# K and V blocks in two transfers of 32 KB runs on two queues, and b1 in one transfer

## The chip, the cores and the metric

The kernel runs on one core of one Trainium2 chip. The metric is device time in microseconds for one execution; the kernel before was timed three times, with a median of 723.58 us (723.52 to 723.64). A profile of one more execution stands beside these times. In it, PE is TensorE's matmul side and PEld its weight loads, DVE is VectorE, ACT ScalarE, POOL GpSimd and SP SyncE; SPq and ACTq are the sequencers of SyncE and ScalarE, which issue transfers. A core has 16 DMA engines, which all transfers share.

## The reference

One decode step, for two sequences (B = 2), of an attention block and an MLP, mixed by a gate. Everything is float32.

```python
def reference(A_x, A_k_cache, A_v_cache, A_wq, A_wo, B_x, B_w1, B_b1, B_w2, B_b2, gate_w):
    x = A_x                                        # (2, 1, 576)
    g = _sigmoid((x * gate_w).sum(-1, keepdims=True))
    a = _A_ref(x, A_k_cache, A_v_cache, A_wq, A_wo)
    b = _B_ref(x, B_w1, B_b1, B_w2, B_b2)
    return g * a + (1 - g) * b

# _A_ref: 32 heads of 128, 4096 cached positions
q = (x @ wq).reshape(B, Sq, H, Dh)                 # then transposed to heads first
scores = einsum("bhqd,bhkd->bhqk", q, k_cache) * (Dh ** -0.5)
o = einsum("bhqk,bhkd->bhqd", softmax(scores), v_cache)
return o.reshape(B, Sq, H * Dh) @ wo

# _B_ref: 576 -> 4608 -> 576
return gelu_tanh(x @ w1 + b1) @ w2 + b2
```

The K cache and the V cache are 134 MB each; the weights are 9.4 MB for wq and for wo, 10.6 MB for w1 and for w2.

## The kernel before

**The blocks.** The 64 pairs of sequence and head are worked off in 16 blocks of four heads of one sequence (NQ = 16, HQ = 4). A block of K or V is 8.39 MB: 128 partitions with 65,536 contiguous bytes each, 32 partitions to a head, 128 positions to a partition. SBUF holds three buffers of that size: slots 0 and 1 take the K blocks in turn, slot 2 takes every V block. At the start and the end the same slots hold the weights.

**What each engine does for a block i.** VectorE multiplies K by the query row in place (L357), sums over the head size (L359, both of some 17 us) and finds the largest score (L360 to L362); this is `qk(i)`. ScalarE takes the exponentials into `pt` (L369, `soft(i)`). TensorE multiplies them by V in 32 steps (L388, in a loop over the blocks). ScalarE copies the sums out of PSUM (L377, into `avs`), TensorE combines them (L393, L395), and ScalarE copies the result into `oS` (L381); these two copies are `gather(i)`.

**Who orders the work.** The order is written out by hand. The class `Order` keeps counting semaphores for each engine and puts waits ahead of an operation (L66, L78); transfers that go through its method `dma` have the line L84. A few semaphores are handled directly: `exps` (exponentials ready), `vin` (V landed), `avd` (V's products done), `avc` and `cmb` (for the two copies), `ksem` (K landed).

**The order of the transfers.** Before the blocks, SyncE issues wq, the rest of wq, and w1 in three pieces. Then comes `k_load(0)`, which loads the first K as two transfers of half a row each, 32,768 bytes to a partition, so that VectorE can begin on the first half; each half has its own semaphore. `k_load(1)` follows when w1 in slot 1 has been used, and the first V when the MLP's activation no longer needs slot 2. In the loop of the blocks SyncE issues K of block i + 2 when `qk(i)` has finished with its slot, and V of block i + 1 when `avd` says that block i is done with slot 2. All of these are single transfers of whole rows on SyncE's queue. The weights w2 and wo follow in the same queue: most of w2 goes into slot 0 ahead of the last V, most of wo and the rest of w2 into slot 1 after the last K has been used, and the last rows of wo into slot 2 after the last V.

**ScalarE's queue** carries only small inputs: x, the gate's weights, b1 and b2 at the start, and half of the output at the end. b1 (4608 numbers, 36 to each of 128 partitions, in `b1T`) comes as 16 transfers of 15, 14, ... 1 and 8 partitions (L142 to L146), which share one semaphore. b2 comes last of these; TensorE needs it to begin the accumulation of the output (L271), ahead of the MLP's first product (L286, L295). The MLP's activation ends with a tanh on ScalarE (L315) and three steps on VectorE, and VectorE then starts on the first K.

Of the kernel before, what the change touches and what calls it, by code (L numbers as in the profile page):

```python
# [9 lines left out]
P = 128  # L10


class Order:
# [50 lines left out]
    def op(self, e, f, r=(), w=(), extra=(), sig=None):  # L64

        self.wait(e, self.deps(r, w) + list(extra))  # L66
        ins = f(self.eng[e])
        if sig is not None:
            ins.then_inc(sig, 1)
            return None  # L70
        self.count[e] += 1
        ins.then_inc(self.sem[e], 1)
        t = self.token(e, self.sem[e], self.count[e])
        self.note(t, r, w)
        return t

    def dma(self, e, out, in_, r=(), w=(), extra=(), sem=None, val=16):
        self.wait(e, self.deps(r, w) + list(extra))  # L78
        if sem is None and self.spare:
            sem, val = self.spare.pop(0)  # L80
        elif sem is None:
            sem = self.tc.alloc_semaphore(f"d{self.nd}")
            self.nd += 1
        self.eng[e].dma_start(out, in_).then_inc(sem, 16)  # L84
        t = (None, sem, val, dict(self.seen[e]))
        self.note(t, r, w)
        return t


def kernel(tc, *args):  # L90
    with tc.tile_critical():
        stored = body(tc, *args)

    with tc.tile_critical():
        for own, sem, val, had in stored:
            tc.nc.sync.wait_ge(sem, val)


def body(tc, x, k_cache, v_cache, wq, wo, w1, b1, w2, b2, gate_w, out):
    nc = tc.nc  # L100
    B, H, SK, DH = k_cache.shape
# [12 lines left out]
    FR = F // P  # L114
# [8 lines left out]
    def sb(name, *shape):  # L123
        return nc.alloc_sbuf_tensor(name, list(shape), F32).ap()

    slots = [sb(f"slot{i}", P, SLOT) for i in range(3)]
# [4 lines left out]
    o = Order(tc)  # L131
    op, dma = o.op, o.dma
    S2 = ["s2a", "s2h", "s2r", "s2t", "xg", "b2r", "xe", "g1z"]


    b1T = sb("b1T", P, FR)
    spare = slots[2][:, 2 * F + 2 * FJ:]
    xg, spare = spare[:B + 1, :D], spare[:, D:]
    b2r, spare = spare[:1, :D], spare[:, D:]
    dma("ACT", xg[:B], x.rearrange("b s d -> (b s) d"), w=["xg"])  # L140
    dma("ACT", xg[B:B + 1], gate_w[None, :], w=["gt_in"])
    b1v, b1sem, at = b1.rearrange("(p r) -> p r", r=FR), tc.alloc_semaphore("b1"), 0  # L142
    b1runs = list(range(15, 0, -1)) + [8]
    for i, n in enumerate(b1runs):
        dma("ACT", b1T[at:at + n], b1v[at:at + n], w=[f"b1T{i}"], sem=b1sem, val=16 * len(b1runs))
        at += n  # L146
    dma("ACT", b2r, b2[None, :], w=["b2r"])


# [6 lines left out]
    dma("SP", slots[2][:, :F], hrow1[:, FA * F:], w=["s2a"])  # L156
    w1h = slots[2][:, F:F + F // 2]
    dma("SP", w1h, w1[XR:].rearrange("q (e n) -> (q e) n", e=2), w=["s2h"])
    early = [o.wrote[k][0][1] for k in ("xg", "gt_in", "b2r", "s0", "s1q", "s1a", "s2a", "s2h")]
    hr = slots[2][:, 2 * F:2 * F + FJ]  # L160
    ht = slots[2][:, 2 * F + FJ:2 * F + 2 * FJ]

    def quad(src, i):
        g, b = divmod(i, B)
        return src[b, g * HQ:(g + 1) * HQ].rearrange("h (p r) d -> (h p) (r d)", p=HP)
# [58 lines left out]
    V = "DVE"  # L224
# [78 lines left out]
    for m, k in enumerate(("avp", "cps", "fin")):  # L303
        op("ACT", lambda e, m=m: e.copy(hr[:, m * FC:(m + 1) * FC], hps[m][:, :FC]), r=[k], w=[f"s2r{m}"])  # L304
    hb = sb("hb", P, FR, B)
# [2 lines left out]
    op(V, lambda e: e.transpose(ht.rearrange("p (r i) -> p r i", i=32), hr.rearrange("p (i r) -> p r i", r=FR)),  # L308
       r=["s2r0", "s2r1", "s2r2"], w=["s2t"])
    htv = ht.rearrange("p (r i) -> p r i", i=32)[:, :, :B]  # L310
    op(V, lambda e: e.tensor_add(hb, htv, b1T.unsqueeze(2).to_broadcast([P, FR, B])), r=["s2t"] + [f"b1T{i}" for i in range(len(b1runs))], w=["hb"])
    op(V, lambda e: e.tensor_mul(gt, hb, hb), r=["hb"], w=["gt"])
    op(V, lambda e: e.tensor_scalar(gt, gt, 0.044715, 1.0, op0=ALU.mult, op1=ALU.add), r=["gt"], w=["gt"])
    op(V, lambda e: e.tensor_mul(gt, gt, hb), r=["gt", "hb"], w=["gt"])
# [14 lines left out]
    vin = tc.alloc_semaphore("vin")  # L329
    avc = tc.alloc_semaphore("avc")  # L330
    avd = tc.alloc_semaphore("avd")
    cmb = tc.alloc_semaphore("cmb")
    ksem = [tc.alloc_semaphore(f"k{j}") for j in range(2)]
    done = lambda sem, val: ("PE", sem, val, {})

    RH = R // 2
    k0b = tc.alloc_semaphore("k0b")

    def k_load(i):
        s = i % 2  # L340
        if i == 0:
            free = o.deps([], ["s0"])
            for a, sem in ((0, ksem[0]), (1, k0b)):
                c = slice(a * RH * DH, (a + 1) * RH * DH)
                dma("SP", slots[0][:, c], quad(k_cache, 0)[:, c], w=[f"s0{a}"], extra=free, sem=sem)
            return
        w = ["s0"] if s == 0 else ["s1a", "s1q", "s1"]
        dma("SP", slots[s], quad(k_cache, i), w=w, sem=ksem[s], val=16 * (i // 2 + 1))

    def qk(i):  # L350
        g, b = divmod(i, B)
        s, j = ("s0", 0) if i % 2 == 0 else ("s1", 1)
        k = slots[i % 2].rearrange("p (r d) -> p r d", d=DH)
        q = qps[b][g // 4][:, (g % 4) * DH:(g % 4 + 1) * DH]
        parts = [(0, R, s)] if i else [(0, RH, "s00"), (RH, R, "s01")]
        for lo, hi, key in parts:
            op(V, lambda e, lo=lo, hi=hi: e.tensor_mul(  # L357
                k[:, lo:hi], k[:, lo:hi], q.unsqueeze(1).to_broadcast([P, hi - lo, DH])), r=["q", key], w=[key])
        op(V, lambda e: e.tensor_reduce(stt[j], k, AX.X, ALU.add), r=[s] + [p[2] for p in parts], w=[f"st{j}"])  # L359
        op(V, lambda e: e.tensor_reduce(mxt, stt[j], AX.X, ALU.max), r=[f"st{j}"], w=["mx"])  # L360
        op(V, lambda e: e.transpose(mtt, mxt.to_broadcast([P, 32])), r=["mx"], w=["mt"])
        op(V, lambda e: e.tensor_reduce(nmt[j], mtt, AX.X, ALU.max, negate=True), r=["mt"], w=[f"nm{j}"])  # L362

    def soft(i):
        j = i % 2
        o.wait("ACT", o.deps([f"nm{j}", f"st{j}"], ["pt", "rs"]))
        for h in range(HQ):
            a = slice(HP * h, HP * (h + 1))
            ins = nc.scalar.activation(pt[a, h:R * HQ:HQ], stt[j][a], AF.Exp, bias=nmt[j][a], accum_out=rs[a])  # L369
        ins.then_inc(exps, 1)  # L370

    def gather(i):

        g, b = divmod(i, B)
        j = i % 2
        nc.scalar.wait_ge(avd, i + 1)
        nc.scalar.copy(avs, avp).then_inc(avc, 1)  # L377
        a = slice(32 * (g // 2), 32 * (g // 2) + 32)
        nc.scalar.wait_ge(cmb, i + 1)

        op("ACT", lambda e: e.copy(oS[a, b, g % 2], cps[a, :DH + 1]), r=[f"st{j}", f"nm{j}"], w=[f"oS{i}"])  # L381

    def quad_products(e, v, vin):
        e.wait_ge(exps, 1).then_inc(exps, -1)
        e.wait_ge(vin, 16).then_inc(vin, -16)  # L385
        for t in range(NT):
            j = t % 4
            ins = e.matmul(avp[32 * j:32 * j + 32], pt[:, 16 * t:16 * t + 32], v[:, 512 * t:512 * (t + 1)],  # L388
                           start=(t < 4), stop=(t >= NT - 4))
        ins.then_inc(avd, 1)  # L390
        e.wait_ge(avc, 1).then_inc(avc, -1)  # L391
        for rr in range(4):
            e.matmul(cps[:, :DH], sel[:, rr], avs[:, rr * DH:(rr + 1) * DH],  # L393
                     start=(rr == 0), stop=(rr == 3), skip_group_check=True)
        e.matmul(cps[:, DH:DH + 1], hsel, rs, start=False, stop=True, skip_group_check=True).then_inc(cmb, 1)  # L395
# [6 lines left out]
    def load_rows(name, lo, hi, s, at, **kw):  # L402
        t = slots[s][:, at * D:(at + hi - lo) * D]
        dma("SP", t, views[name][:, lo * D:hi * D], w=[(name, lo)], **kw)
        for r in range(lo, hi):
            wrow[name, r] = t[:, (r - lo) * D:(r - lo + 1) * D], (name, lo)


    k_load(0)
    k_load(1)  # L410
    o.wait("SP", o.deps([], S2 + ["gt_in", "s2r0", "s2r1", "s2r2"]))
    nc.sync.dma_start(slots[2], quad(v_cache, 0)).then_inc(vin, 16)
    for i in range(NQ):
        qk(i)
        if i < NQ - 2:
            k_load(i + 2)
        elif i < N1:
            o.spare = [(sem, 32) for sem in early]
            load_rows("w2", 0, WA, 0, 0, extra=o.deps([], ["s0"]))
        soft(i)  # L420
        if i < N1:
            gather(i)
            nc.sync.wait_ge(avd, i + 1)
            nc.sync.dma_start(slots[2], quad(v_cache, i + 1)).then_inc(vin, 16)
    o.wait("PE", o.deps(["sel0", "sel1", "sel2", "sel3", "hsel", "pt"], ["avp", "cps"]))
    with nc.Fori(0, NQ, engines=[PE], head_slot={PE: 0}):
        quad_products(nc.tensor, slots[2], vin)
# [41 lines left out]
    for gp in range(2):  # L469
# [11 lines left out]
       r=["orr", "rg"], w=["oT"])  # L481
# [89 lines left out]
```

## Time and profile before

| | |
|---|---|
| time, median of 3 | 723.58 us (723.52 to 723.64) |
| time of the profiled execution | 723.66 us |
| its span | 721.8 us |
| busy, VectorE | 598.7 us |
| busy, TensorE | 220.0 us |
| busy, ScalarE | 49.6 us |
| moved | 308.69 MB, 428 GB/s over the span |
| packets | 6912 |

The span reaches from the first to the last instruction; the rest of an execution's time lies around it. The row "DMA" of the page cuts the span into 40 slices, and each digit is the busy share of the 16 DMA engines in tenths, 9 for 90% and more. Below it, a row for each queue tells its packets, its megabytes and the time that its packets took as a share of 16 engines' time. q1 is SyncE's queue, q10 ScalarE's; q8 and q14 fetch instructions and tables. A packet is one contiguous run of one partition, or the 4-byte write with which an engine raises a transfer's semaphore. The DMA view can be asked for a stretch of the span, and then counts the packets that start in it. A row of the timeline has the start and the duration in us, then engine, line, operation and tiles, and in brackets how long the engine was idle before and what ended that.

### The profile page before, as it was taken

What the parts mean: (1) busy time and instruction counts of PE and PEld (TensorE: products, weight loads), DVE (VectorE), ACT (ScalarE), POOL (GpSimd) and SP (SyncE); (2) the same over time, 40 slices, a digit from 0 to 9 for tenths busy, and PEclk for the clock granted to TensorE, in tenths of its full rate; (3) what the DMA queues carried; (4) which work ended last, traced back from release to release, by engine and by line L of the source; (5) the groups of instructions that cost most, each with busy time, mean ns of one, the idle gap of its engine ahead of it and who ended that gap; (6) DMA issues with size and microseconds to landing.
All of it is one profiled execution on the core that took longest, in us unless ns stands there. A gap on an engine that the chain in (4) does not pass through costs nothing. (4 is left out here: it accounts for less than half of the span.)

```text
span 721.8 us, 4007 instructions
## 1 busy us (share of the span) xinstructions
PE 220.0 (30%) x1720; PEld 78.7 (11%) x1720; DVE 598.7 (83%) x162; ACT 49.6 (7%) x166; POOL 0.7 (0%) x6
## 2 busy tenths in 40 slices
PE   1764005050504132140505060504032140506076
PEld 1221002020101010010102020101001010102022
DVE  2004999999999898989899898989898989899860
ACT  0000010101010101010100001010101010100000
POOL 0000000000000000000000000000000000000000
PEclk9988557575666657575757575666657575757579
DMA  9999999999999999999999999999999999999996
GB/s 407 409 414 456 418 454 418 454 418 451 410 447 425 432 436 421 450 421 450 421 447 425 447 414 447 425 425 443 421 450 421 447 425 447 425 439 425 447 401 273
DMA packets 6912, 308.69 MB, mean 428 GB/s; under 512 B 1004, under 2 KB 1012, under 8 KB 1400
## 3 DMA queue, kind: packets, MB, share of 16 engines
q1 hardware_dynamic: 6632, 308.55, 99.0%
q8 instruction: 5, 0.08, 0.0%
q10 hardware_dynamic: 272, 0.03, 0.0%
q14 instruction: 3, 0.02, 0.0%
HBM read 308.57 MB, written 0.00 MB: 428 GB/s over the span
## 5 line engine op out<-in xcount | busy, mean ns | idle before, releaser
L357 DVE TENSOR_TENSOR slot<-slot,bank 128x16384 f32<-128x16384 f32 (+1 forms) x17 | 275.6, 16214 | 36.4 <-DMA slot<-in_A_k_cache_dram 36.4
L388 PE MATMUL bank<-slot,pt 128*32 128x512 f32 x1024 | 150.3, 753 | 457.1 <-PEq L385 457.1
L359 DVE TENSOR_REDUCE st<-slot 128x128 f32<-128x16384 f32 x16 | 275.5, 17220 | 0.5
L388 PEld LDWEIGHTS bank<-slot,pt 128*32 128x32 f32 x1024 | 41.1, 134 | 553.7 <-issue 553.7
L369 ACT ACTIVATE pt<-st,nm 32x128 f32<-32x128 f32 x64 | 33.0, 515 | 125.0 <-DVE nm L362 120.7
L377 ACT COPY avs<-bank 128x512 f32<-128x512 f32 x16 | 9.4, 586 | 441.0 <-PE bank L388 441.0
L308 DVE STREAM_TRANSPOSE slot<-slot 128x1152 f32<-128x1152 f32 x1 | 2.2, 2202 | 44.9 <-ACT slot L304 44.9
L454 DVE SCALAR_TENSOR_TENSOR slot<-slot,hg 128x576 f32<-128x576 f32 x34 | 24.9, 814 | 0.0
L393 PE MATMUL bank<-avs,sel 128*128 128x128 f32 x128 | 18.1, 284 | 12.7 <-PEq L391 12.7
L245 PE MATMUL bank<-slot,xq 128*32 128x512 f32 x160 | 18.7, 630 | 8.1 <-DMA slot<-in_A_wq_dram 8.1
L393 PEld LDWEIGHTS bank<-avs,sel 128*128 128x128 f32 x128 | 15.5, 191 | 26.8 <-issue 26.8
L369 ACT ACTIVATION_READ_ACCUMULATOR pt<-st,nm 32x1 f32 x64 | 12.5, 195 | 0.0
L286 PE MATMUL bank<-slot,xT 128*32 128x384 f32 x96 | 9.4, 557 | 0.0
L520 DVE COPY pt<-bank 128x288 f32<-128x288 f32 x1 | 0.5, 457 | 10.7 <-PE bank L489 10.7
L489 PE MATMUL bank<-slot,oT 128*2 128x288 f32 x108 | 7.3, 406 | 1.3 <-DMA slot<-in_A_wo_dram 0.8
L180 DVE COPY slot<-slot 3x64 f32<-3x64 f32 x2 | 0.4, 184 | 8.7 <-DMA slot<-in_gate_w_dram 8.6
L245 PEld LDWEIGHTS bank<-slot,xq 128*32 128x32 f32 x160 | 5.0, 117 | 21.0 <-issue 12.8
L381 ACT COPY oS<-bank 32x129 f32<-32x129 f32 x16 | 4.1, 258 | 22.8 <-PE bank L395 22.8
L470 DVE TENSOR_TENSOR avs<-oS,dm 128x256 f32<-128x256 f32 x2 | 0.8, 422 | 5.6 <-ACT oS L381 5.6
L489 PE MATMUL bank<-slot,hg 128*2 128x288 f32 x72 | 5.4, 406 | 0.0
L360 DVE TENSOR_REDUCE mx<-st 128x1 f32<-128x128 f32 x16 | 4.6, 286 | 0.5
L395 PEld LDWEIGHTS bank<-rs,hsel 128*128 128x128 f32 x32 | 4.9, 192 | 0.0
(65 smaller groups left out, 48.1 us busy)
## 6 DMA issues: line engine op xcount, KB each, us to landing
slot<-in_A_k_cache_dram SPq DMA_DIRECT2D x2, 4096.0 KB, 27.5
slot<-in_B_w_dram SPq DMA_DIRECT2D x1, 8064.0 KB
slot<-in_B_w_dram SPq DMA_DIRECT2D x1, 6912.0 KB, 41.3
slot<-in_A_wo_dram SPq DMA_DIRECT2D x1, 5184.0 KB
slot<-in_B_w_dram SPq DMA_DIRECT2D x2, 2304.0 KB, 46.3
slot<-in_A_wo_dram SPq DMA_DIRECT2D x1, 1440.0 KB, 11.6
slot<-in_B_w_dram SPq DMA_DIRECT2D x1, 1152.0 KB, 48.5
slot<-in_A_wo_dram SPq DMA_DIRECT2D x1, 1152.0 KB, 14.0
```

The lines of the kernel that those rows point to most:

```text
L245: ins = e.matmul(qps[b][m][HP * h:HP * (h + 1)], xq[:, c, b:b + 1].to_broadcast([P, HP]), v[:, :, h], start=(c == 0), stop=last, skip_grou ...
L286: ins = e.matmul(hps[m][32 * j:32 * j + 32, :FC], xT[:, c], t[:, at:at + FC], start=(c == 0), stop=False, skip_group_check=True)
L357: op(V, lambda e, lo=lo, hi=hi: e.tensor_mul(k[:, lo:hi], k[:, lo:hi], q.unsqueeze(1).to_broadcast([P, hi - lo, DH])), r=["q", key], w=[key])
L359: op(V, lambda e: e.tensor_reduce(stt[j], k, AX.X, ALU.add), r=[s] + [p[2] for p in parts], w=[f"st{j}"])
L360: op(V, lambda e: e.tensor_reduce(mxt, stt[j], AX.X, ALU.max), r=[f"st{j}"], w=["mx"])
L369: ins = nc.scalar.activation(pt[a, h:R * HQ:HQ], stt[j][a], AF.Exp, bias=nmt[j][a], accum_out=rs[a])
L377: nc.scalar.copy(avs, avp).then_inc(avc, 1)
L388: ins = e.matmul(avp[32 * j:32 * j + 32], pt[:, 16 * t:16 * t + 32], v[:, 512 * t:512 * (t + 1)], start=(t < 4), stop=(t >= NT - 4))
L393: e.matmul(cps[:, :DH], sel[:, rr], avs[:, rr * DH:(rr + 1) * DH], start=(rr == 0), stop=(rr == 3), skip_group_check=True)
L395: e.matmul(cps[:, DH:DH + 1], hsel, rs, start=False, stop=True, skip_group_check=True).then_inc(cmb, 1)
L454: op(V, lambda e: e.scalar_tensor_tensor(wacc[:, b], t, hg[:, r, b:b + 1], wacc[:, b], op0=ALU.mult, op1=ALU.add), r=[key, "hg", f"wacc{b} ...
L489: ins = e.matmul(acc[64 * s + 32 * u:64 * s + 32 * u + B], lhs, t[:, u * DW:(u + 1) * DW], start=False, stop=last, skip_group_check=True)
```

## The change

Every K and V block but the first K comes as two transfers. SyncE issues the first half of every partition's row, ScalarE the second half, with the same wait each; both raise the same semaphore, so what waits for it now waits for 32 (on `ksem[0]`, which the first K's first half raises by 16, for 16 plus 32 for each later block). The new function `halves` does this. ScalarE's halves stand in its program where the code calls `halves`: K's half ahead of `soft(i)`, V's half behind `gather(i)`. The first K, the weights and the output are left as they were. b1 comes as one transfer of 128 partitions; its semaphore joins those that are used again later on.

```diff
-    b1v, b1sem, at = b1.rearrange("(p r) -> p r", r=FR), tc.alloc_semaphore("b1"), 0
-    b1runs = list(range(15, 0, -1)) + [8]
-    for i, n in enumerate(b1runs):
-        dma("ACT", b1T[at:at + n], b1v[at:at + n], w=[f"b1T{i}"], sem=b1sem, val=16 * len(b1runs))
-        at += n
+    dma("ACT", b1T, b1.rearrange("(p r) -> p r", r=FR), w=["b1T"])
     dma("ACT", b2r, b2[None, :], w=["b2r"])
...
+    def halves(a, b, out, src, sem, free):
+
+        for j, e in enumerate((a, b)):
+            c = slice(j * RH * DH, (j + 1) * RH * DH)
+            o.wait(e, free)
+            o.eng[e].dma_start(out[:, c], src[:, c]).then_inc(sem, 16)
+
     def k_load(i):
...
         w = ["s0"] if s == 0 else ["s1a", "s1q", "s1"]
-        dma("SP", slots[s], quad(k_cache, i), w=w, sem=ksem[s], val=16 * (i // 2 + 1))
+        free = o.deps([], w)
+        halves("SP", "ACT", slots[s], quad(k_cache, i), ksem[s], free)
+        val = 16 + 32 * (i // 2) if s == 0 else 32 * (i // 2 + 1)
+        o.note((None, ksem[s], val, {}), (), w)
...
-        e.wait_ge(vin, 16).then_inc(vin, -16)
+        e.wait_ge(vin, 32).then_inc(vin, -32)
...
-    o.wait("SP", o.deps([], S2 + ["gt_in", "s2r0", "s2r1", "s2r2"]))
-    nc.sync.dma_start(slots[2], quad(v_cache, 0)).then_inc(vin, 16)
+    halves("SP", "ACT", slots[2], quad(v_cache, 0), vin, o.deps([], S2 + ["gt_in", "s2r0", "s2r1", "s2r2"]))
...
             gather(i)
-            nc.sync.wait_ge(avd, i + 1)
-            nc.sync.dma_start(slots[2], quad(v_cache, i + 1)).then_inc(vin, 16)
+            halves("SP", "ACT", slots[2], quad(v_cache, i + 1), vin, [done(avd, i + 1)])
```

More of the change, by code (lines that the diff above doesn't have):

```diff
@@ L158, in body @@
     dma("SP", w1h, w1[XR:].rearrange("q (e n) -> (q e) n", e=2), w=["s2h"])
-    early = [o.wrote[k][0][1] for k in ("xg", "gt_in", "b2r", "s0", "s1q", "s1a", "s2a", "s2h")]
+    early = [o.wrote[k][0][1] for k in ("xg", "gt_in", "b1T", "b2r", "s0", "s1q", "s1a", "s2a", "s2h")]
     hr = slots[2][:, 2 * F:2 * F + FJ]
@@ L310, in body @@
     htv = ht.rearrange("p (r i) -> p r i", i=32)[:, :, :B]
-    op(V, lambda e: e.tensor_add(hb, htv, b1T.unsqueeze(2).to_broadcast([P, FR, B])), r=["s2t"] + [f"b1T{i}" for i in range(len(b1runs))], w=["hb"])
+    op(V, lambda e: e.tensor_add(hb, htv, b1T.unsqueeze(2).to_broadcast([P, FR, B])), r=["s2t", "b1T"], w=["hb"])
     op(V, lambda e: e.tensor_mul(gt, hb, hb), r=["hb"], w=["gt"])
```

## The prediction

> **What bounds the kernel now.** I read the page first, for who is busy.
>
> ```profile
> PE 220.0 (30%) x1720; PEld 78.7 (11%) x1720; DVE 598.7 (83%) x162; ACT 49.6 (7%) x166; POOL 0.7 (0%) x6
> DMA  9999999999999999999999999999999999999996
> q1 hardware_dynamic: 6632, 308.55, 99.0%
> q10 hardware_dynamic: 272, 0.03, 0.0%
> ```
>
> VectorE is busy for 83% of the span, but the packets of SyncE's queue (q1) fill 99.0% of the time of all 16 DMA engines, and no slice but the last falls under nine tenths. ScalarE's queue (q10) carries next to nothing. So 721.8 us of span hold 714.6 us of packets, and the rest is start and end. A change of the time must come out of those packets, or out of a new hole between them.
>
> The end of the chain that ended last agrees:
>
> ```profile
> 689.91 9.52 PE bank L388 x64
> 701.24 16.36 DMA slot<-in_A_wo_dram
> 717.64 0.47 PE bank L534 x8
> 718.14 0.31 DVE pt L538
> ```
>
> What it waits for last is a 16.36 us stretch of transfers of wo; after them come 0.8 us of work and the store. Next I asked how full the engines are where only whole K and V blocks move, by the DMA view of 300 to 600 us:
>
> ```profile
> DMA packets 2240, 130.02 MB, mean 433 GB/s; under 512 B 256, under 2 KB 256, under 8 KB 256
> q1 hardware_dynamic: 2240, 130.02, 100.1%
> ```
>
> 256 of the 2240 packets are the small ones that raise semaphores; the other 1984 carry 65,536 bytes each (130.02 MB). They fill 100.1%: no hole at all, and a record overlaps the next one a little. How far the queue is from running dry is read from SyncE's timeline and VectorE's, inside one period:
>
> ```profile
> 389.49 0.33 SPq L424 DMA_DIRECT2D slot<-in_A_v_cache_dram  x1
> 395.64 0.33 SPq L84 DMA_DIRECT2D slot<-in_A_k_cache_dram  x1
> 429.32 0.33 SPq L424 DMA_DIRECT2D slot<-in_A_v_cache_dram  x1
> 434.34 0.33 SPq L84 DMA_DIRECT2D slot<-in_A_k_cache_dram  x1
> ...
> 399.83 17.22 DVE L357 TENSOR_TENSOR slot<-slot,bank 128x16384 f32<-128x16384 f32 x1 [3.43 <-DMA slot<-in_A_k_cache_dram]
> ```
>
> K follows K after 38.70 us, which is sixteen 64 KB packets on each engine (eight for K, eight for V), 2.419 us each. When V is issued at 389.49, the K ahead of it still has until 399.83 to land: 10.3 us of work are queued. At the K issue there is that K's rest and a whole V. VectorE waits 3.43 us in a period for data, so it has slack and the transfers have none.
>
> **The change part by part: more packets.** 31 whole-block transfers (16 of V, 15 of K; the first K has come as two halves already) become 62 of 32 KB runs. On each engine 31 x 8 = 248 packets of 64 KB become 496 of 32 KB, for the same bytes. What does a packet cost beside its bytes? The only 32 KB packets of before are those of the first K; this is the DMA view of 57 to 67 us, inside that transfer:
>
> ```profile
> DMA packets 145, 4.21 MB, mean 421 GB/s; under 512 B 16, under 2 KB 16, under 8 KB 16
> q1 hardware_dynamic: 144, 4.19, 97.4%
> ```
>
> 128 of them carry data. 97.4% of 160 engine-us is 155.84 us; less some 0.2 us for the 16 small ones, 1.216 us for each. The 64 KB packet: 100.1% of 4800 is 4804.8 us, less some 2.5 us for 256 small ones, over 1984: 2.4205 us. Two 32 KB packets thus take 2.432 us, 12 ns more than one of 64 KB. A third size, the 18 KB rows of w2 at 701 to 705 us, tells whether that is a fixed cost or an accident of the first K:
>
> ```profile
> q1 hardware_dynamic: 97, 1.71, 100.3%
> ```
>
> 93 packets of 18,432 bytes take 64.19 us, 0.690 us each. From 18 KB to 64 KB the time rises by 1.7305 us for 47,104 bytes, so 65,536 bytes alone are 2.408 us and a packet's own cost is 12 to 13 ns, the same figure as from the halves. It is fixed, by these rows. The records overlap, though: 0.1% of 300 us over the 124 data packets of one engine is 2.4 ns (1.2 to 3.6 with the rounding). An added packet costs 12 less about 2 to 4: I take 9 ns. 248 x 9 ns = 2.2 us. Each added transfer also brings one semaphore packet an engine: 31 at under 10 ns, 0.3 us. The bounds for the 9 ns are 5 (the rounding of both shares against me, and a part hidden) and 14 (rounding for it, no overlap): 1.2 to 3.5 us.
>
> The Trainium skill, page "DMA: Bandwidth & Descriptors", section "Why small descriptors are slow (HBM only)", speaks of a fixed overhead of about 3 cycles per packet and of 32 bytes of metadata per operation; at the 850 MHz that this page gives for the fabric that is, as an estimate, some 4.7 ns, and 248 of them would be 1.2 us, half of my term. The rows above say 9 and I go by them.
>
> **Two queues.** Where the halves stand in the program decides whether an engine can find both queues empty. ScalarE before, from tanh on through the first block; names are those of the code, pt the exponentials, avs and oS copies of the sums:
>
> ```order
> L315 ACTIVATE gt<-gt 128x72 [waits cDVE]
> L369 ACTIVATE pt,rs<-st,nm 32x128 [waits cDVE]
> L369 ACTIVATE pt,rs<-st,nm 32x128 x3
> L377 COPY avs<-bank 128x512 [waits avd]
> L381 COPY oS<-bank 32x129 [waits cmb]
> ```
>
> ScalarE in the changed program, the same place:
>
> ```order
> L311 ACTIVATE gt<-gt 128x72 [waits cDVE]
> L340 DMA slot<-in_A_k_cache_dram 128x8192
> L340 DMA slot<-in_A_v_cache_dram 128x8192
> L340 DMA slot<-in_A_k_cache_dram 128x8192 [waits cDVE]
> L375 ACTIVATE pt,rs<-st,nm 32x128 [waits cDVE]
> L375 ACTIVATE pt,rs<-st,nm 32x128 x3
> L383 COPY avs<-bank 128x512 [waits avd]
> L387 COPY oS<-bank 32x129 [waits cmb]
> L340 DMA slot<-in_A_v_cache_dram 128x8192 [waits avd]
> ```
>
> What moved: ScalarE now issues K's half ahead of the exponentials, and V's half behind both copies; SyncE issues its half of V as soon as avd comes. On SyncE no row moves; whole rows become halves in place. The two copies on ScalarE now:
>
> ```profile
> 429.32 0.59 ACT L377 COPY avs<-bank 128x512 f32<-128x512 f32 x1 [30.77 <-PE bank L388]
> 431.34 0.26 ACT L381 COPY oS<-bank 32x129 f32<-32x129 f32 x1 [1.43 <-PE bank L395]
> ```
>
> So ScalarE's half of V goes out at 431.60, 2.3 us after SyncE's at 429.32. Ten us of the K before it stand in both queues then, so this costs nothing; were that cover gone, SyncE's half would still run alone at full rate, and an engine stands idle only when both are empty. The exponentials wait behind one issue of 0.33 us; they are ready long before V. What is late next is nothing: V's products wait for V, and V for its turn.
>
> At the start there is more to watch. The rows of b1 are one small packet after another in ScalarE's queue:
>
> ```profile
> 1.79 5.93 ACTq L84 DMA_DIRECT2D b1T<-in_B_b_dram  x16
> 7.74 0.27 ACTq L84 DMA_DIRECT2D slot<-in_B_b_dram  x1
> 47.84 2.25 PE L271 MATMUL bank<-slot 1*128 1x288 f32 x4 [6.11 <-DMA slot<-in_B_b_dram]
> 57.60 0.33 SPq L84 DMA_DIRECT2D slot<-in_A_k_cache_dram  x1
> 65.25 0.33 SPq L412 DMA_DIRECT2D slot<-in_A_v_cache_dram  x1
> 66.98 17.28 DVE L357 TENSOR_TENSOR slot<-slot,bank 128x8192 f32<-128x8192 f32 x2
> 101.53 0.33 SPq L84 DMA_DIRECT2D slot<-in_A_k_cache_dram  x1
> ```
>
> b2, issued at 7.74 behind 16 transfers, reaches TensorE at 47.84: 40.1 us over 16 is 2.5 us, one 64 KB packet for each. So an engine takes one packet of one queue, then one of the other, and does not lose time by it. With b1 in one transfer, eight rows an engine instead of sixteen on the fullest, b2 lands earlier; TensorE's 6.11 us of waiting goes, and the second K and first V are issued up to 6 us sooner. That is worth nothing while the first K is still in the queue. ScalarE saves some 5.6 us of issues before its first work, for which nobody waits. The packets of b1 weigh 0.0% of the engines: nothing, within 0.1 us either way.
>
> But ScalarE's halves of the second K and first V, issued behind tanh at about 60 to 66, now share the engines with the second half of the first K, which SyncE still has in its queue. When would that half have landed? The view of V has its longest landing, which is the first V's:
>
> ```profile
> DMA to landing us min/median/max: 28.3/29.1/44.3
> ```
>
> 65.25 + 44.3 = 109.55 is the end of three blocks in a row; two blocks of 8 x 2.419 = 19.35 us before that, the first K ended, at 70.85. At equal shares its last 5 to 8 us take twice as long, and it lands at 75 to 79. VectorE, which starts on the first half at 66.98 or up to 6 us sooner and needs 8.6 us for it, then waits up to 4 us more for the second, and the K that was issued at 101.53 goes out by 105. The queues hold work until about 108, so nothing is lost, with 3 to 6 us to spare. At the end, ScalarE's last half of V shares with w2 and wo, which SyncE has queued; same bytes, same end.
>
> **The sum.** 2.2 + 0.3 + 0 + 0 = +2.5 us. The profiled execution took 723.66 us (span 721.8), 0.08 over the median 723.58, so 723.58 + 2.5 = 726.1 us, slower by 0.35%. About 0.2% (1.45 us) is what a measurement can tell from no change here.
>
> **The rivals.** (1) Hidden cost: with a second queue filled, an engine prepares the next packet of one queue while it moves the other's, and most of the 9 ns vanishes. Then only the semaphore packets and up to half the 9 ns are left: 0.3 to 1.4 us, 723.9 to 725.0, about 724.5. For it: the trace has no two bulk queues at once. Against it: 64 KB packets one behind the other in one queue, prefetched as well as can be, pay it too. The skill's 4.7 ns would also end here, near 725.0. 17%.
>
> (2) Faster: alternation hides the cost of all packets, not only of the added ones. Each 64 KB then takes its bytes alone, 2.408 us in place of 2.419: 248 x 11 ns = 2.7 us less, 0.3 more for semaphores, 721.2 us. It decides from 6 ns a packet gained on. Against it stands that the engines are at 100.1% with one queue, and that b1's alternation gained nothing visible. 5%. The skill's same page, section "Issuing engines are not separate DMA queues", says that transfers run on the same 16 engines whoever issues them and that only issue time is saved; the 100.1% agrees.
>
> (3) A hole at the start: the engines favour ScalarE's queue, and the first K's second half lands behind both ScalarE halves, 19 us late at about 90. VectorE would end the block near 116 instead of 101.53, 6 to 8 us after the queues are empty, and no later slack gives that back: 726.1 + 7 = 733. It starts to cost when that half lands after about 82. The one-to-one alternation of b1 speaks against it. 6%.
>
> **How the numbers follow.** The forecast has 72%; its own range is 725.1 to 727.4 (1.2 to 3.5 us and the semaphores). Rival 1 gives 17% within 0.2%, and 2% of the forecast, at its lowest end, falls there as well: same 0.19, faster 0.05, slower 0.70 + 0.06 = 0.76. The range of 724.3 to 727.8 leaves out rivals 2 and 3 and less than half of rival 1; its upper 0.4 us are the smallest holes that rival 3 could leave.
>
> **What would show it.** Right: q10 carries 130 MB (31 x 4.19) and q1 178 MB; the spacing of K issues grows from 38.70 to about 38.85 us; the data packets of 300 to 600 us are of 32 KB and still fill 100% of the engines; TensorE no longer waits for b2. The spacing is the cleanest: 38.70 or less means rival 1 or 2. A stretch under full share near 100 to 125 us means rival 3. The forecast is wrong if the spacing stays and the time moves, or if the spacing grows by more than 0.25 us.

## The result and the profile after

The changed kernel takes 726.60 us (median of 6, 725.90 to 727.12) against 723.55 for the kernel before (723.42 to 723.64): a ratio of 1.0042, 95% interval 1.0029 to 1.0055. That is 3.05 us slower. In a second series on another occasion it took 727.30 us (726.38 to 727.71) against 723.63, ratio 1.0049 (1.0035 to 1.0063). Its runs scatter over 1.2 and 1.3 us, those of the kernel before over 0.2 and 0.3.

The page after has the same engines as full as before, and the bytes on two queues:

```profile
DMA packets 11264, 308.69 MB, mean 426 GB/s; under 512 B 1388, under 2 KB 1396, under 8 KB 1784
...
q1 hardware_dynamic: 6632, 178.53, 57.4%
q10 hardware_dynamic: 4624, 130.06, 41.7%
```

11,264 packets stand where 6,912 stood, for the same 308.69 MB, and the two shares add up to 99.1%. The DMA view of 300 to 600 us, the steady stretch, gives:

```profile
DMA packets 4464, 129.50 MB, mean 432 GB/s; under 512 B 512, under 2 KB 512, under 8 KB 512
...
q10 hardware_dynamic: 2232, 64.75, 50.2%
q1 hardware_dynamic: 2232, 64.75, 50.1%
```

3952 packets of 32 KB fill 100.3% of the engines with 129.5 MB; before, 1984 of 64 KB filled 100.1% with 130.0. K now follows K on SyncE's timeline after 38.85 and 38.86 us, where it was 38.70:

```profile
398.75 0.33 SPq L340 DMA_DIRECT2D slot<-in_A_k_cache_dram  x1
432.48 0.33 SPq L340 DMA_DIRECT2D slot<-in_A_v_cache_dram  x1
437.60 0.33 SPq L340 DMA_DIRECT2D slot<-in_A_k_cache_dram  x1
470.68 0.33 SPq L340 DMA_DIRECT2D slot<-in_A_v_cache_dram  x1
476.46 0.33 SPq L340 DMA_DIRECT2D slot<-in_A_k_cache_dram  x1
```

0.155 us more in a period is, over sixteen added packets and two added semaphore packets on each engine, 8.6 to 9.7 ns a packet. The 31 added transfers are 15.5 periods, so this accounts for 2.4 of the 3.05 us. The end of the chain is what it was, three microseconds later:

```profile
693.07 9.44 PE bank L394 x64
...
704.32 16.16 DMA slot<-in_A_wo_dram
```

What is left, 0.65 us and the scatter, must come from elsewhere. The start of the blocks looks different. The rows are TensorE's, ScalarE's, SyncE's and VectorE's, from the timeline:

```profile
43.14 1.23 PE L267 MATMUL bank<-slot 1*128 1x288 f32 x4
...
58.81 0.36 ACTq L340 DMA_DIRECT2D slot<-in_A_k_cache_dram  x1
59.20 1.20 ACTq L340 DMA_DIRECT2D slot<-in_A_v_cache_dram  x1
...
61.23 8.69 DVE L363 TENSOR_TENSOR slot<-slot,bank 128x8192 f32<-128x8192 f32 x1 [1.40 <-DMA slot<-in_A_k_cache_dram]
...
79.36 8.69 DVE L363 TENSOR_TENSOR slot<-slot,bank 128x8192 f32<-128x8192 f32 x1 [9.44 <-DMA slot<-in_A_k_cache_dram]
...
105.33 0.33 SPq L340 DMA_DIRECT2D slot<-in_A_k_cache_dram  x1
```

TensorE no longer waits for b2 (43.14 for 47.84), and VectorE starts 5.75 us sooner. Then it waits 9.44 us for the second half of the first K, which shares the engines with ScalarE's two halves, and the third K goes out at 105.33 for 101.53.

### The profile page after: what moved, and what is told of

Its sections match the earlier page's. It is cut to its first block, busy times and chain, and to the rows that moved or that the text cites. A ratio compares the mean times of both kernels' runs of the same rounds, so it can differ in the third digit from the quotient of the medians.

```text
span 724.6 us, 4023 instructions
## 1 busy us (share of the span) xinstructions
PE 213.8 (30%) x1720; PEld 77.3 (11%) x1720; DVE 598.9 (83%) x162; ACT 49.6 (7%) x166; POOL 0.7 (0%) x6
## 2 busy tenths in 40 slices
DMA packets 11264, 308.69 MB, mean 426 GB/s; under 512 B 1388, under 2 KB 1396, under 8 KB 1784
## 5 line engine op out<-in xcount | busy, mean ns | idle before, releaser
L394 PE MATMUL bank<-slot,pt 128*32 128x512 f32 x1024 | 145.3, 731 | 472.4 <-PEq L391 472.4
L241 PE MATMUL bank<-slot,xq 128*32 128x512 f32 x160 | 20.2, 671 | 8.0 <-DMA slot<-in_A_wq_dram 8.0
L399 PEld LDWEIGHTS bank<-avs,sel 128*128 128x128 f32 x128 | 15.5, 191 | 26.8 <-issue 26.8
L282 PE MATMUL bank<-slot,xT 128*32 128x384 f32 x96 | 7.9, 487 | 0.0
L401 PE MATMUL bank<-rs,hsel 128*128 128x1 f32 x32 | 4.5, 210 | 0.0
```

What stands on the lines that cost most here:

```text
L241: ins = e.matmul(qps[b][m][HP * h:HP * (h + 1)], xq[:, c, b:b + 1].to_broadcast([P, HP]), v[:, :, h], start=(c == 0), stop=last, skip_grou ...
L282: ins = e.matmul(hps[m][32 * j:32 * j + 32, :FC], xT[:, c], t[:, at:at + FC], start=(c == 0), stop=False, skip_group_check=True)
```

## The experiments

Theory P, from the prediction, says that the time comes from packets: 248 more on each engine, at some 9 ns each. Rival Q says that it comes from two queues with bulk data on the same engines. Every kernel here has b1 in one transfer unless the text says otherwise.

**b1 alone.** The kernel before with the change of b1, and nothing of K and V.

```diff
-    for i, n in enumerate(b1runs):
-        dma("ACT", b1T[at:at + n], b1v[at:at + n], w=[f"b1T{i}"], sem=b1sem, val=16 * len(b1runs))
-        at += n
+    dma("ACT", b1T, b1.rearrange("(p r) -> p r", r=FR), w=["b1T"])
```

> The kernel before with b1 in one transfer, nothing else. Theory P (price of a packet: the time comes from 248 more data packets on each engine) expects no change: 723.5 us, within 0.3, since the DMA engines carry the same large packets; b2 reaches TensorE some 18 us after the start and the second K and the first V are issued up to 7 us sooner, without use. A rival B (part of the loss comes from b1: sixteen rising transfers left the last engines free, one even transfer does not) expects 0.3 to 0.7 us more, 723.9 to 724.3.

Measured: 723.46 us (723.29 to 724.00), ratio 1.0000 (0.9991 to 1.0008). The third K goes out almost 5 us sooner, and nothing comes of it:

```profile
96.89 0.33 SPq L84 DMA_DIRECT2D slot<-in_A_k_cache_dram  x1
```

Alone, b1's transfer shows no cost and no gain; the interval reaches 0.6 us either way. The median and all but one of the runs lie below theory B's 723.9 to 724.3, so B falls, though the interval alone would still allow its lower end.

**Halves on one queue.** The changed kernel with SyncE issuing both halves.

```diff
-        halves("SP", "ACT", slots[s], quad(k_cache, i), ksem[s], free)
+        halves("SP", "SP", slots[s], quad(k_cache, i), ksem[s], free)
```

V likewise.

> The changed kernel with both halves of every K and V on SyncE's queue. Theory P expects the loss to stay for the most part: the same 496 packets of 32 KB on each engine, 723.55 + 2.2 + 0.2 = 725.9 us, spacing of K issues 38.85 us; the half microsecond that is left to 726.6 would be a hole near 107 us in the changed kernel, where the second queue delays the first K (theory H), and be gone here. Rival Q (what costs is two queues with bulk data sharing the engines) expects the time of before, 723.5, and a spacing of 38.70.

Measured: 725.87 us (725.80 to 726.02), ratio 1.0033 (1.0020 to 1.0046), 2.32 us over the kernel before. The DMA view of 300 to 600 us, and SyncE's timeline:

```profile
DMA packets 4450, 129.57 MB, mean 432 GB/s; under 512 B 496, under 2 KB 496, under 8 KB 496
...
q1 hardware_dynamic: 4450, 129.57, 100.3%
```

```profile
435.77 0.80 SPq L340 DMA_DIRECT2D slot<-in_A_k_cache_dram  x2
...
474.63 0.80 SPq L340 DMA_DIRECT2D slot<-in_A_k_cache_dram  x2
```

One queue alone keeps the engines at 100.3%, and the spacing is 38.86 us all the same, with 129.57 MB where two queues moved 129.50. Three quarters of the loss need no second queue. Q is wrong about the steady stretch.

**Quarters, on two queues and on one.** Four transfers of 16 KB runs for each K and V.

```diff
-        for j, e in enumerate((a, b)):
-            c = slice(j * RH * DH, (j + 1) * RH * DH)
+        for j, e in enumerate((a, b, a, b)):
+            c = slice(j * RH * DH // 2, (j + 1) * RH * DH // 2)
```

On two queues:

> The changed kernel with each K and V in four transfers of 16 KB runs, two on each queue. Theory P expects three times the added packets, 3 x 2.2 = 6.6 us, and 0.6 us of semaphore packets, with or without 0.5 us of the hole: 730.7 to 731.3 us, spacing near 39.1 to 39.2. Rival Q expects no more than the changed kernel, 726.6, since the queues are the same two.

Measured: 736.32 us (730.66 to 740.31), ratio 1.0160 (1.0126 to 1.0195), above what either expected, with a scatter of 10 us. SyncE's timeline:

```profile
590.95 0.80 SPq L340 DMA_DIRECT2D slot<-in_A_v_cache_dram  x2
596.21 0.80 SPq L340 DMA_DIRECT2D slot<-in_A_k_cache_dram  x2
630.99 0.80 SPq L340 DMA_DIRECT2D slot<-in_A_v_cache_dram  x2
635.78 0.33 SPq L84 DMA_DIRECT2D slot<-in_B_w_dram  x1
675.42 0.80 SPq L340 DMA_DIRECT2D slot<-in_A_v_cache_dram  x2
```

V follows V after 40.0 us, and then, once w2 stands in SyncE's queue, after 44.4. The last V is late, and the engines run out of work before the last weights can be asked for. Whether these 5 us need the second queue was tested by the same quarters on SyncE's queue alone (the edit is that of the halves on one queue):

> Four transfers of 16 KB runs for every K and V, all on SyncE's queue. Theory P expects 3 x 2.2 + 0.6 = 7.2 us, so 730.7 us, with little scatter. If the extra 5 us of the quarters on two queues came from the sharing at the end, they are gone here; if short packets cost more than theory P says, the time stays near 736.

Measured: 730.59 us (730.50 to 730.65), ratio 1.0096 (1.0081 to 1.0112). The expectation was 730.7. K's issues on SyncE's timeline are 39.15 us apart:

```profile
399.02 1.75 SPq L340 DMA_DIRECT2D slot<-in_A_k_cache_dram  x4
433.34 1.75 SPq L340 DMA_DIRECT2D slot<-in_A_v_cache_dram  x4
438.17 1.75 SPq L340 DMA_DIRECT2D slot<-in_A_k_cache_dram  x4
```

6.96 us for three times the added packets, 2.32 for the single measure: the price of a packet is the same from 64 to 32 and from 32 to 16 KB, 9.4 ns with its share of the semaphores. P holds in amount. The rest of the quarters' loss belongs to two queues, and the packets of the two traces, with each packet's bytes spread evenly over its time, show where: by 660 us both have moved the same bytes, by 680 the two queues are 1.5 us of work behind, by 720 5.1 us. So it lies wholly at the end, where V shares with the weights. Its likely cause is that by turns, packet for packet, w2's rows of 64,512 bytes get four times the bytes of a 16 KB packet: from 654 to 662 us SyncE's queue starts 43 packets of w2 and ScalarE's 49 of V. No run tests that by itself.

**Whole rows on two queues.** Two trials of a second queue without added data packets. The first splits by partition:

```diff
-            c = slice(j * RH * DH, (j + 1) * RH * DH)
-            o.eng[e].dma_start(out[:, c], src[:, c]).then_inc(sem, 16)
+            c = slice(j * P // 2, (j + 1) * P // 2)
+            o.eng[e].dma_start(out[c], src[c]).then_inc(sem, 16)
```

> The changed kernel with the split by partition: SyncE loads partitions 0 to 63, ScalarE 64 to 127, in whole rows of 64 KB. Two queues, but no more data packets than before; only the 31 added semaphore packets on each engine. Theory P expects 723.55 + 0.2 to 0.3 = 723.8 us, or 724.3 if the hole near 107 us (theory H) is there as well, and a spacing of 38.71. Rival Q expects 726 to 726.6 and a spacing near 38.85.

Measured: 1349.13 us (1295.83 to 1359.67). Neither theory had this, and the run says nothing between them. The DMA view of 300 to 600 us, from the run of 1295.83 us:

```profile
DMA packets 1264, 65.95 MB, mean 220 GB/s; under 512 B 256, under 2 KB 256, under 8 KB 256
...
q10 hardware_dynamic: 638, 33.42, 50.9%
q1 hardware_dynamic: 624, 32.51, 49.3%
```

1008 packets of 64 KB fill the engines; each takes 4.77 us, twice the 2.42 of a transfer to 128 partitions. Why is open: no run has transfers to 64 partitions on one queue. The second trial leaves transfers whole and gives the queues blocks by turns:

```diff
-        dma("SP", slots[s], quad(k_cache, i), w=w, sem=ksem[s], val=16 * (i // 2 + 1))
+        dma(("SP", "ACT")[s], slots[s], quad(k_cache, i), w=w, sem=ksem[s], val=16 * (i // 2 + 1))
```

V of block i likewise on SyncE for even i, on ScalarE for odd.

> Whole rows of 64 KB again, b1 in one transfer, but two queues: K and V of the even blocks on SyncE, of the odd blocks on ScalarE. No packet is added. Theory P expects the rate of before in full stretches (64 KB packets of 2.42 us) and a time of 723.5 us, plus at most 1 to 1.5 us if the shared engines leave a hole at the start or the end, below 725. Rival Q (two queues with bulk data cost of themselves) expects 726 or more with the engines full and each packet longer.

Measured: 738.89 us (738.13 to 740.25), ratio 1.0217 (1.0202 to 1.0233). P's time is missed, and so is Q's reason. In the steady stretch the rate is that of before, 1984 data packets and 130.02 MB in 300 us at 100.2%:

```profile
DMA packets 2224, 130.02 MB, mean 433 GB/s; under 512 B 240, under 2 KB 240, under 8 KB 240
...
q1 hardware_dynamic: 1134, 66.98, 51.6%
q10 hardware_dynamic: 1090, 63.05, 48.6%
```

Over half of the loss is at the start. In the windows, whose last two columns are the engines' share and the GB/s, the engines stand idle:

```profile
105.00:110.00 5.00, 0.00 (x0) 0.00 (x0) 5.00 (x1) 0.00 (x0) 0.00 (x0) 0.50 0.24 105
110.00:115.00 5.00, 0.00 (x0) 0.00 (x0) 4.90 (x5) 0.17 (x1) 0.00 (x0) 0.50 0.04 13
```

```profile
88.07 8.69 DVE L353 TENSOR_TENSOR slot<-slot,bank 128x8192 f32<-128x8192 f32 x1 [17.95 <-DMA slot<-in_A_k_cache_dram]
...
114.04 0.33 SPq L84 DMA_DIRECT2D slot<-in_A_k_cache_dram  x1
```

The second K, whole on ScalarE's queue, took turns with the first K's second half, which VectorE then had only at 88.07. From 107.3 to 109.5 us one engine after another ran out of packets, and the third K, which waits for VectorE, was not asked for until 114.04. By its packets this trace is 8.0 us of work behind that of before at 120 us, and still 7.9 us at 705. The rest of the 14.5 us by which its span is longer is lost at the end, where the last rows of wo are issued at 715.97 and not at 699.45, likely since the last V, on ScalarE's queue, shares with SyncE's weights.

The hole at the start is that of rival 3 of the prediction, with the first K at 88 for the 90 expected there. It suggests where the changed kernel's last 0.7 us are.

**The start on one queue.** Theory H: the halves of ScalarE delay the first K, the third goes out late, and a small hole follows near 107 us. From the changed kernel:

```diff
-        halves("SP", "ACT", slots[s], quad(k_cache, i), ksem[s], free)
+        halves("SP", "SP" if i == 1 else "ACT", slots[s], quad(k_cache, i), ksem[s], free)
```

The first V has both halves on SyncE as well.

> The changed kernel, but the second K and the first V come with both halves on SyncE's queue; from the third K and second V on one half each stays on ScalarE's. Theory H (the half microsecond by which the changed kernel is slower than the same halves on one queue comes from the start, where ScalarE's halves delay the first K, the third K goes out late, and the engines find their queues all but empty near 107 us) expects 725.9 us, within 0.3, little scatter from run to run, and full engines from 105 to 120 us. Rival S (it is the steady sharing of the engines by two queues, or the end, where ScalarE's half of V shares with w2) expects 726.4 to 726.8 as in the changed kernel.

The changed kernel stood beside it:

> The changed kernel once more, beside the others on the same chip: 726.6 us with the scatter seen before, 725.9 to 727.1, by every theory.

Measured: 729.75 us (728.88 to 730.38), ratio 1.0088 (1.0074 to 1.0102), slower than the changed kernel's 727.30. As put, H fails. The third K did go out early, at 96.75, but a hole opened later, in SyncE's timeline and the windows:

```profile
96.75 0.33 SPq L340 DMA_DIRECT2D slot<-in_A_k_cache_dram  x1
...
128.02 0.33 SPq L340 DMA_DIRECT2D slot<-in_A_v_cache_dram  x1
```

```profile
125.00:130.00 5.00, 4.21 (x38) 1.87 (x30) 5.00 (x1) 0.59 (x1) 0.00 (x0) 1.00 0.64 229
```

Of the first V's 8.4 MB, 3.3 still stood in SyncE's queue when the packets of ScalarE's half of the third K began to take turns with them, at 100.2 us. So V was late (TensorE begins on it at 119.45 us, in the changed kernel at 110.98), the second V went out at 128.02 (119.64 in the changed kernel), and the engines were at 64% meanwhile.

**In step, or in time?** Two theories remained. D: the queues must carry the same blocks from the first K on. M: all that counts is how long before the queues run dry the next block is asked for. For D, the second half of the first K went on ScalarE's queue, ahead of its copies of the MLP:

```diff
+    dma("ACT", slots[0][:, c1], quad(k_cache, 0)[:, c1], w=["s01"], extra=o.deps([], ["s0"]), sem=k0b)
```

> The changed kernel with the second half of the first K on ScalarE's queue, ahead of its copies of the MLP, so that both queues carry the same blocks from the first K on. Theory D (the queues are out of step at the start: ScalarE's has nothing of the first K, runs half a block ahead, and a block is then late just when the queues are short of work) expects what the halves cost on one queue, 725.9 to 726.2 us with a scatter below 0.5, and full engines from 100 to 130 us. Rival S (the steady sharing or the end costs the rest) expects 726.6 to 727.3 as in the changed kernel.

Measured: 727.25 us (726.02 to 728.26), ratio 1.0053 (1.0039 to 1.0066). D fails. Both halves land together now, VectorE starts only at 70.93, and the third K is late again:

```profile
70.93 17.29 DVE L364 TENSOR_TENSOR slot<-slot,bank 128x8192 f32<-128x8192 f32 x2 [1.41 <-DMA slot<-in_A_k_cache_dram]
```

```profile
105.50 0.33 SPq L342 DMA_DIRECT2D slot<-in_A_k_cache_dram  x1
```

With it ran the changed kernel with b1 in its sixteen transfers again (the first diff above, backwards):

> The changed kernel with b1 in its sixteen transfers again. The MLP then ends some 7 us later, and ScalarE's first halves of K and V are issued near 66 instead of 59 us, when the first K is nearly through. Theory D expects the queues less out of step: 726.0 to 726.4 us, a smaller hole near 107 us than the changed kernel's. A rival on which b1 only helps, or does nothing, expects 726.6 to 727.3 or more.

Measured: 726.10 us (725.89 to 726.63), ratio 1.0033 (1.0021 to 1.0045), the time that D had expected, though D fell with the run before.

```profile
102.71 0.33 SPq L344 DMA_DIRECT2D slot<-in_A_k_cache_dram  x1
```

The third K goes out sooner than in the changed kernel (105.33). So b1, which does nothing alone, moves the changed kernel's start: with it in one transfer ScalarE's halves come while more of the first K is outstanding. The intervals of this kernel and the changed one overlap; their scatter, 0.7 against 1.2 and 1.3 us, tells more.

The last two put M to the test from both sides. One keeps both queues and makes ScalarE wait for the first K before it issues its first halves:

```diff
     k_load(0)
+    o.wait("ACT", o.wrote["s01"])
     k_load(1)
```

> The changed kernel, but ScalarE waits until the whole first K has landed before it issues its halves of the second K and first V; b1 in one transfer as before this edit. Nothing delays the first K then, and the third K goes out near 97 us, 10 us ahead of the end of the first V. Theory M (margin: what the changed kernel loses beyond its packets, 0.7 to 1.3 us, comes from the third K being issued at 105 to 106 us, less than 2 us before the engines have finished all that was queued) expects what the halves cost on one queue, 725.8 to 726.2 us, scatter below 0.7, and no hole from 100 to 130 us. Rival S (two queues of themselves) expects 726.6 to 727.3 with the same scatter as the changed kernel.

The other has one queue and makes the third K late, by letting VectorE begin the first block when all of it has landed:

```diff
-        parts = [(0, R, s)] if i else [(0, RH, "s00"), (RH, R, "s01")]
+        parts = [(0, R, s)] if i else [(0, R, "s01")]
+        if i == 0:
+            o.wait("DVE", o.wrote["s00"])
```

> Both halves of every K and V on SyncE's queue, as in the second experiment (725.87 us), but VectorE begins the first block only when the whole first K is there, one multiplication instead of two. The third K then goes out near 105 us. Theory M expects the changed kernel's loss on one queue alone: a hole near 107 us, 726.3 to 727.3, more scatter than 725.80 to 726.02. Rival S expects no loss, 725.9, since there is but one queue.

Measured: two queues in time, 726.22 us (725.97 to 726.24), ratio 1.0036 (1.0022 to 1.0050); one queue late, 726.53 us (726.17 to 727.15), ratio 1.0042 (1.0028 to 1.0055). The loss and the scatter went with the late issue and not with the second queue. The third K in the first and in the second of them:

```profile
97.14 0.33 SPq L340 DMA_DIRECT2D slot<-in_A_k_cache_dram  x1
```

```profile
105.43 0.80 SPq L340 DMA_DIRECT2D slot<-in_A_k_cache_dram  x2
```

What a late issue does to the engines shows best with one queue; the DMA view of 104 to 112 us, first of the halves on one queue, then of the late one:

```profile
DMA packets 119, 3.38 MB, mean 422 GB/s; under 512 B 16, under 2 KB 16, under 8 KB 16
...
q1 hardware_dynamic: 119, 3.38, 98.0%
```

```profile
DMA packets 107, 2.98 MB, mean 373 GB/s; under 512 B 16, under 2 KB 16, under 8 KB 16
...
q1 hardware_dynamic: 107, 2.98, 97.1%
```

The share of the engines hardly falls, but 0.40 MB less have moved, 0.9 us of work: some packets take longer. Of the late kernel's 91 data packets here 24 take over 1.3 us, up to 2.75; none of the other's 103 does. So this hole is hardly seen in the busy share, only in the bytes and in the packets' times. All kernels with halves, in the order of the third K's issue:

| kernel | third K issued, us | median, us | range, us |
|---|---|---|---|
| halves on one queue | 96.97 | 725.87 | 725.80 to 726.02 |
| ScalarE waits for the first K | 97.14 | 726.22 | 725.97 to 726.24 |
| changed, b1 in sixteen | 102.71 | 726.10 | 725.89 to 726.63 |
| changed | 105.33 | 726.60 | 725.90 to 727.12 |
| one queue, late | 105.43 | 726.53 | 726.17 to 727.15 |
| first K on both | 105.50 | 727.25 | 726.02 to 728.26 |
| changed, second series | 106.41 | 727.30 | 726.38 to 727.71 |

The issue times are those of the profiled executions. Their packets, with the bytes of each spread evenly over its time, give what is lost between 106 and 112 us, as an estimate against the halves on one queue: nothing in the second and third rows, then 0.34 us in the changed kernel, 0.97 in the late one, 0.44 with the first K on both queues, and 0.69 in the changed kernel's second series. In that second series this is all of the 0.70 us by which the profiled execution is longer than that of the halves on one queue; in the first series it is half of 0.71, and the other half shows only after 717 us, at the very end, for a reason that is open. The start on one queue (96.75, 729.75 us) is not in the table, since there V was the late block.

## Why the prediction was right, and where it was off

**The price of a packet was right.** The forecast took 9 ns, from the rows of the first K's halves and of w2, and 2.5 us with the semaphore packets. The halves on one queue measured 2.32 us, the quarters 6.96 for three times as much. The spacing of K's issues was forecast at 38.85 us and came at 38.85 and 38.86. The estimate of 1.2 us from the figures of the Trainium skill ("DMA: Bandwidth & Descriptors", section "Why small descriptors are slow (HBM only)") would have been half of the 2.32 us. Rival 1 (the cost is hidden by a second queue) is refuted by the equal spacing on one queue and on two, rival 2 by the sign.

**Two queues cost nothing in a full stretch**, as the forecast said: 129.50 MB in 300 us on two and 129.57 on one. The Trainium skill ("DMA: Bandwidth & Descriptors", section "Issuing engines are not separate DMA queues") says that transfers run on the same 16 engines and interleave, whichever engine issued them; the two byte counts agree. ScalarE's later half of V, 2.0 us behind SyncE's, cost nothing there either.

**What failed is the step on the start.** It said that the third K goes out by 105, that the queues hold work until about 108, and "so nothing is lost, with 3 to 6 us to spare". The issue was foreseen (105.33), and the wait for the first K was undersized: VectorE waited 9.44 us for its second half, since the half landed just behind 79 and VectorE had begun near 61. (The "up to 4 us" goes with a start at 66.98; with the 6 us sooner that the same sentence allows, its own figures give up to 9.4.) The error is in what such a margin is worth. The end that it put at 108 is spread over the engines: with blocks by turns, the first of them ran out at 107.3 us and the last at 109.5, so the issue at 105.33 was about 2 us ahead of the first, and not 3 to 6. That is not enough; at 102.71 the hole was gone. The changed kernel, whose start was set at nothing, takes 0.7 us more than the halves on one queue in the first series and 1.4 in the second, and varies from run to run; the traces place 0.34 and 0.69 us of it in this hole. It is rival 3's hole in the small, without rival 3's cause: no queue was favoured. The first K's second half landed just behind 79, at the upper end of the 75 to 79 of equal shares and ahead of the 82 from which rival 3 was to cost.

**b1 was right alone and wrong in company.** Nothing came of it in the kernel before. In the changed kernel it brings ScalarE's first halves ahead by about 8 us (59 for 67), into the first K, and the third K goes out at 105 rather than 103.

What stays open: why packets stretch when the next block is asked for late, how the scatter arises, and where the rest of the first series' 0.7 us goes. The runs show only that the stretched packets and the scatter go with the late issue.

## What to carry to other kernels

When the DMA engines are full from end to end, count packets: here each one cost 9 ns beside its bytes, at 32 KB and at 16 KB, and the trace of before prices it, from two sizes of packets in stretches where nothing waits. Here a second issuing queue added no rate to full engines, but it changed which transfer finished first; look for the block that the next issue depends on, and ask what now shares the engines with it. Check the margin at the thinnest place, which here was the start, and the end in the quarters and the blocks by turns, and not in the steady period.

## What the runs showed of the hardware

With two transfers to 64 partitions each, side by side on two queues, the data moved at half the rate of transfers to 128, with all engines busy: 4.77 us for a 64 KB packet in place of 2.42, and 220 GB/s in place of 433. The queues' packets take turns one for one, so the larger packet gets more bytes. The blocks by turns show it from 63 to 83 us, where ScalarE's queue has packets of 64 KB and SyncE's of 32 KB:

```profile
q10 hardware_dynamic: 83, 5.44, 62.8%
q1 hardware_dynamic: 80, 2.62, 30.4%
```

The 5.7 us between the quarters on two queues and on one fit that, but no run isolates it. Engines may be fully busy by their share and still move less: 97.1% and 373 GB/s in the late kernel, 98.0% and 422 in the other.
